# A limit of four filter rows under way in the loads of a convolution that runs beside attention

## The chip, the cores and the metric

The kernel runs on one core of a Trainium2 chip. The core has a matrix engine (TensorE, PE in the profile; its weight loads are PEld), a vector engine (VectorE, DVE), a scalar engine (ScalarE, ACT), a general engine (GpSimd, POOL) and a sequencer that here only issues transfers (SyncE, SP). SBUF is the memory on the core, PSUM the accumulators of TensorE, HBM the main memory. Transfers between HBM and SBUF (DMAs) are issued by SP, ACT or POOL and carried by 16 DMA engines. Each engine takes its own instructions in order; engines wait for one another, and for DMAs, on semaphores.

The metric is the device time of one execution in microseconds. The time before is 860.05 us, the median of three runs (854.38 to 860.23). The profile comes from one more execution, which took 848.04 us.

## The reference

Two independent blocks are computed on inputs of 2048 x 512 in bfloat16 and set side by side in the output. Block A is attention with 32 heads of width 16. Block B is a gated long convolution: a short filter of four taps, a product, then for each of 512 channels a causal convolution over all 2048 positions, done in the reference with an FFT.

```python
def _A_ref(x, wqkv, wo):
    ...
    scores = jnp.einsum("bhqd,bhkd->bhqk", q, k) * (Dh ** -0.5)
    p = _softmax(scores, axis=-1)
    o = jnp.einsum("bhqk,bhkd->bhqd", p, v)
    return (lambda x, *d: x.transpose(*d))(o, 0, 2, 1, 3).reshape(B, S, D) @ wo

def _B_ref(q, k, v, shift_k, ssm_k, ssm_D):
    ...
    kv = k_shift * v
    ...
    y_f = kv_f * kf_f[None, :, :, :]
    y = (lambda x, s, axes=(-2,-1): jnp.fft.irfft2(x, s=s, axes=axes).astype(jnp.bfloat16))(y_f, (1, L), axes=(1, 2))[:, 0, :S, :]
    y = y + kv * ssm_D[None, None, :]
    return q * y

a = _A_ref(A_x, A_wqkv, A_wo)
b = _B_ref(B_q, B_k, B_v, B_shift_k, B_ssm_k, B_ssm_D)
return jnp.concatenate([a, b], axis=-1)
```

## The kernel before

Both blocks run at the same time on the same core, interleaved in one long order of instructions for each engine. A planner in the source, written in Python, makes that order ahead of time: it carries a model of how long everything takes and appends an instruction to an engine's list when the model says that it fits. What the chip then runs is fixed; only the waits on semaphores decide when each instruction starts.

**Attention.** Scores are made in blocks of 128 keys by 512 queries. TensorE multiplies queries and keys (L787, contraction over 32 rows of the array, three blocks at a time), ACT takes the exponential of two or three blocks in one instruction from PSUM to the tile PT (L794), and TensorE multiplies the result with the values (L862). A part of the blocks has its exponential worked out on DVE and POOL by a polynomial instead (L813, L822, L823). Steps are numbered T; each step has one score group, one exponential, and whatever else fits on TensorE before the exponential of that step ends.

**Convolution.** For every channel d the filter, reversed and padded with 128 zeros, is written once at the start to a scratch area in HBM, kz_scratch, as a row of 2176 elements. A *filter row* in SBUF is made from it by one DMA of 128 x 2048 elements: partition p gets the same row shifted by p elements (a Toeplitz matrix). This is `load_wr`, and the tile WR holds a ring of R_W = 14 such rows, slot d % 14. The products k_shift * v lie in the tile KV. TensorE works on four channels at once (a *quad*, qd): for each of 16 lags of 128 positions it makes four matmuls of 128 x 128, one for each channel, in four column groups of the array (`conv_lags`, L988). A quad is therefore 64 matmuls and reads four filter rows; 128 quads make the block. A quad is cut into pieces of up to six lags that the planner puts between the attention's matmuls.

**How the rows are loaded.** The first 14 rows are loaded while the products are made, as WR's memory, which holds other data at first, comes free. After that `conv_lags` issues four loads when it has put the last lag of a quad: the slots of the four rows that this quad has read go to the rows 14 places on. The load is issued from SP and waits until TensorE has finished the quad (`h_wrfree`). Each slot has a semaphore of its own, d_wr[r], and `h_wr[d]` is the handle of row d's landing; the first matmuls of a quad wait for its four rows. From the end of the start phase to the end of the kernel SP has nothing else to issue than these loads, and two stores of the output at the very end. Loads and stores of other tiles (the projection weights WOP, the gate input QN, the outputs) go through POOL. The planner models when a row lands only by numbers of its own (`state["wr"]`), not by the handles of the loads.

Of the kernel before, what the change touches and what calls it, by code (L numbers as in the profile page):

```python
# [28 lines left out]
R_W = 14  # L29
# [5 lines left out]
BGB = 7  # L35
N_EARLY = 70
LAGS = 6

# [131 lines left out]
def bass_concat_heads__mha_block__ssm_conv_h3__prompt_kernel(  # L172
# [163 lines left out]
    def at_job(j):  # L336
        return at_of(j.h) if isinstance(j, Job) and j.h is not None else math.inf if isinstance(j, Job) else at_of(j)
# [23 lines left out]
    def dma(eng, dsem, outp, inp, deps=(), transpose=False):  # L361
        h = dsem.add()

        def fn(e):
            f = e.dma_start_transpose if transpose else e.dma_start
            f(outp, inp).then_inc(dsem.sem, 16)  # L366
        eng.op(fn, deps, inc=False)
        return h
# [221 lines left out]
    def kv_chunk(j):  # L590
        b = kvbuf[kv_buf[j]]
        st = {}

        def tap(m):
            in1 = TB[:, m:m + 1, :].broadcast_to([128, 2, D])
            st[m] = dve_job(lambda e: e.tensor_tensor(b[m], b[m], in1, ALU.mult),
                            [h_kv[(j, 0)], h_kv[(j, 1)], h_tb[m]], 750.0, 3000.0)

        def add(m):
            st["a"] = dve_job(lambda e: e.tensor_tensor(b[3], b[3], b[m], ALU.add), [st[m], st[3], st.get("a")], 750.0, 3500.0)  # L600

        def last():
            def then(h):
                h_kvfree[j] = h
                nxt = {4: 1, 3: None, 2: 0}.get(j, j - 3)
                if nxt is not None and nxt >= 0:
                    load_kv(nxt)
                for d in {6: (0, 1), 5: (2, 3), 4: (4, 11), 3: (8, 9, 12, 13), 1: (5, 6, 7)}.get(j, ()):
                    load_wr(d, [h])
                if j == 5:  # L610
                    load_qn(0, [h_kzt[0]], 4, NB)
                    line[0] += 5000.0
                elif j == 0:
                    start_conv(h)
            for i in range(2):
                dve_job(lambda e, i=i: e.tensor_tensor(KV[:, :, NB - 1 - 2 * j - i, :], quads(b[3][:, i, :]), quads(b[4][:, i, :]), ALU.mult),  # L616
                        [st["a"], h_xt[0]], 700.0, 4000.0 + i, then if i else None)
        return [lambda m=m: tap(m) for m in (3, 2)] + [lambda: add(2), lambda: tap(1), lambda: add(1),
                                                       lambda: tap(0), lambda: add(0), last]

    h_kzw = [None]
# [340 lines left out]
    h_wr, h_wrfree, h_qn = {}, {}, {}  # L962
    h_yb, h_yb_in = {}, {}

    def load_wr(d, deps=()):
        r = d % R_W
        deps = [h_kzw[0], *deps] if d < R_W else [h_wrfree[d - R_W]]
        if d < R_W:
            line[0] += 1350.0
        src = bass.AP(tensor=kz_ap.tensor, offset=kz_ap[d, 0].offset, ap=[[1, 128], [1, S]])  # L970
        h_wr[d] = dma(sp, d_wr[r], WR[:, r, :], src, deps)
# [5 lines left out]
    def conv_lags(qd, n0, n1):  # L977
# [16 lines left out]
        if n1 == NB:  # L994
            for c in range(4):
                h_wrfree[4 * qd + c] = h
                if 4 * qd + c + R_W < C:
                    load_wr(4 * qd + c + R_W)
            if kk % 4 == 3:
                half = kk // 4  # L1000
                src = PS[:, BGB, :]
                src = bass.AP(tensor=src.tensor, offset=PS[:, BGB, 127:128].offset,
                              ap=[src.ap[0], [128, 4], [-1, 128]])
                bank_free[BGB] = dve_job(lambda e: e.tensor_copy(YB[:, half, :].rearrange("p (k i) -> p k i", k=4), src),  # L1004
                                         [h, (lambda: h_yb.get(qd // 8 - 1, WAIT)) if qd >= 8 else None])
                h_yb_in[qd // 4] = bank_free[BGB]
# [41 lines left out]
    def start_conv(h):  # L1048
        h_kvc[0] = h
        state["started"] = True  # L1050
        load_wr(10, [h])
        load_qn(0, [h], 0, 4)
        now = at_of(h)
        state["dma"] = max(line[0], now) + 5000.0
        state["wr"] += [now - 1000.0, max(line[0], now) + 2000.0, state["dma"] - 1400.0]
        state["dma"] -= 1400.0
# [36 lines left out]
    def fill(t, limit):  # L1093
        if t + 450.0 < limit and at_job(bank_free[BGB]) <= t:
            state["fill"] += 2
            bank_free[BGB] = pe_op(keep_busy, [bank_free[BGB]], full(512, 2))
# [27 lines left out]
    def emit_lags(T):  # L1124
# [19 lines left out]
        ahead = [(st["wr"][i] + 1500.0 - now) / (NB * (i - st["qd"]) - st["lag"]) for i in range(st["qd"] + 1, len(st["wr"]))]  # L1144
        st["lags"] = min(st["lags"] + (now - st["now"]) / max([PACE] + ahead), 2.0 * LAGS)
        st["now"] = now
        lags = LAGS
        while st["qd"] < C // 4:
# [3 lines left out]
            if n0 == 0 and (st["wr"][st["qd"]] + 1000.0 > t or st["qd"] % 4 == 0 and at_job(bank_free[BGB]) > t):  # L1152
                if st["qd"] % 4 == 0 and lags == LAGS:
                    fill(t, limit)
# [211 lines left out]
```

## Time and profile before

| What | us |
|---|---|
| Median of three runs | 860.05 |
| Lowest and highest of them | 854.38, 860.23 |
| Profiled execution | 848.04 |
| Its span, first to last instruction | 846.3 |

A page of the profile shows the whole execution: the busy time of each engine, the span in 40 slices with the traffic of the DMA engines in each (21.2 us to a slice), the DMA queues with their bytes, the chain of work that ended last, the costliest groups of instructions (each with what its engine waited for just before), and the DMA issues with the time from issue to landing. Other views ask the same trace more closely: the waits of one engine, the instructions on one tile or one source line, a table of busy time for chosen stretches, and the instructions in order of time.

The queue that carries the filter rows is SP's. What SP itself waited for stands in the view of its waits; the columns are the total in us, how often, and the longest:

```profile
SPq L366 <- PE PS L988: 285.6, 79, 7.0
SPq L366 <- PE PS L1112: 100.2, 26, 6.7
SPq L366 <- PE PS L787: 59.8, 16, 5.9
```

All three are the same wait, for TensorE to be done with a quad (L366 is the line of the helper that issues every DMA). The view names the instruction of PE that came last, whichever line it has. No wait of SP for a filter row is in the program before.

### The profile page before, as it was taken

The numbers are of one execution on the slowest core, as the hardware profiler recorded it, in microseconds if no ns is written. First come the engines' busy times: TensorE is split into PE (matmuls) and PEld (weight loads), VectorE is DVE, ScalarE is ACT, GpSimd is POOL, SyncE is SP. The second block draws the span as 40 slices with busy tenths as digits, with TensorE's granted clock in tenths as the row PEclk, the third lists the DMA queues.
The fourth block names the chain that finished last, engine by engine and source line by source line (L and its number), as shares of the span: only waits on it lengthen the run. The fifth ranks groups of instructions, "written<-read, shape, count | busy, mean of one in ns | idle before, by whom it ended". The sixth has DMA issues, their size and how long they took to land.

```text
span 846.3 us, 30017 instructions
## 1 busy us (share of the span) xinstructions
PE 710.1 (84%) x13188; PEld 308.1 (36%) x13232; DVE 799.7 (94%) x1342; ACT 820.7 (97%) x732; POOL 284.4 (34%) x317
## 2 busy tenths in 40 slices
PE   8988988888888878888788888887888888887887
PEld 3322233433333333333333333333333333343332
DVE  3888999999999999999999999999999999999996
ACT  6999999999999999999999999999999999999997
POOL 3221332333333333233333433334233333323331
PEclk9999999999999999999999999999999999999999
DMA  9868589999999999999999999999999999999942
GB/s 313 301 192 294 174 302 334 367 409 406 391 365 352 399 361 377 387 394 324 409 408 343 350 357 407 406 403 391 354 397 380 378 407 375 372 393 391 388 148 75
DMA packets 88436, 295.69 MB, mean 349 GB/s; under 512 B 11126, under 2 KB 19315, under 8 KB 87923
## 3 DMA queue, kind: packets, MB, share of 16 engines
q1 hardware_dynamic: 82386, 280.00, 88.3%
q0 software_dynamic: 3776, 12.58, 4.4%
q8 instruction: 105, 1.72, 0.8%
q10 hardware_dynamic: 2144, 1.18, 0.5%
q14 instruction: 25, 0.20, 0.1%
HBM read 287.31 MB, written 6.42 MB: 347 GB/s over the span
## 4 chain that ended last, share of the span: by engine, by line
ACT 62%; DVE 23%; PE 11%; issue 2%; DMA 1%; ACTq 0%
ACT PT L794 62%; DVE PTD L823 5%; DVE EI L813 5%; DVE EM L822 5%; PE PS L787 4%; DVE WKV L822 4%; PE PS L862 2%; PE PS L519 1%; DVE QT L540 1%; PE PS L988 1%; DMA WKV<-in_A_wqkv_dram 1%; DVE DT L888 1%; PE PS L505 1%; PE PS L512 1%; PE PS L936 1%
## 5 line engine op out<-in xcount | busy, mean ns | idle before, releaser
L794 ACT ACTIVATE PT<-PS 128x1024 bf16<-128x1024 f32 (+1 forms) x726 | 817.2, 1348 | 13.8 <-PE PS L787 12.8
L787 PE MATMUL PS<-QT,KTo 32*128 32x512 bf16 x2048 | 285.7, 386 | 116.3 <-ACT PT L794 96.9
L988 PE MATMUL PS<-WR,KV 128*8 128x128 bf16 (+15 forms) x8192 | 251.5, 220 | 4.4 <-issue 3.9
L988 PEld LDWEIGHTS PS<-WR,KV 128*1 128x1 bf16 (+15 forms) x8192 | 167.2, 87 | 84.3 <-issue 43.7
L289 POOL TENSOR_SCALAR WKV<-EI 128x512 f32<-128x512 uint16 x128 | 123.6, 965 | 221.1 <-DVE EM L822 85.6
L289 POOL TENSOR_SCALAR EM<-EI 128x512 f32<-128x512 uint16 x128 | 123.1, 962 | 219.4 <-DVE WKV L822 90.1
L862 PE MATMUL PS<-PT,VAF 128*32 128x512 bf16 x1792 | 187.8, 391 | 1.6 <-issue 1.1
L813 DVE TENSOR_SCALAR EI<-PS 128x512 int32<-128x512 f32 x256 | 173.5, 678 | 4.0 <-PE PS L787 3.8
L787 PEld LDWEIGHTS PS<-QT,KTo 32*128 32x128 bf16 x2048 | 71.9, 91 | 276.2 <-ACT PT L794 224.3
L822 DVE SCALAR_TENSOR_TENSOR WKV<-WKV 128x512 f32<-128x512 f32 x256 | 171.0, 680 | 1.1 <-POOL WKV L289 0.7
L822 DVE SCALAR_TENSOR_TENSOR EM<-EM 128x512 f32<-128x512 f32 x256 | 170.9, 686 | 0.2
L823 DVE SCALAR_TENSOR_TENSOR PTD<-EI,WKV 128x512 uint16<-128x512 int32 x128 | 87.2, 682 | 0.6
L823 DVE SCALAR_TENSOR_TENSOR PTD<-EI,EM 128x512 uint16<-128x512 int32 x128 | 86.9, 680 | 0.6
L862 PEld LDWEIGHTS PS<-PT,VAF 128*32 128x32 bf16 x1792 | 47.2, 93 | 105.9 <-issue 98.6
L862 PE MATMUL PS<-PTD,VAF 128*32 128x512 bf16 x256 | 76.4, 387 | 0.6
L1112 PE MATMUL PS<-IDN,ZER 128*32 128x512 bf16 x428 | 48.1, 383 | 0.0
L888 DVE STREAM_TRANSPOSE DT<-PS 128x512 f32<-128x512 f32 x31 | 22.1, 711 | 6.4 <-PE PS L862 5.7
L862 PEld LDWEIGHTS PS<-PTD,VAF 128*32 128x32 bf16 x256 | 19.1, 94 | 18.5 <-DVE PTD L823 8.8
L540 DVE TENSOR_TENSOR QT<-PS,MSK 128x1024 bf16<-128x1024 f32 x15 | 18.4, 1224 | 5.7 <-PE PS L505 5.5
L1004 DVE CAST YB<-PS 128x512 bf16<-128x512 f32 x32 | 21.7, 678 | 0.7 <-PE PS L988 0.5
L366 POOL DMA_DIRECT2D WR<-in_B_k_dram x15 | 11.0, 737 | 27.2 <-DVE KV L616 18.7
L366 POOL DMA_DIRECT2D out_dram<-OUTA x12 | 7.1, 593 | 36.1 <-DVE OUTA L948 36.1
(79 smaller groups left out, 301.2 us busy)
## 6 DMA issues: line engine op xcount, KB each, us to landing
WR<-kz_scratch SPq DMA_DIRECT2D x512, 512.0 KB, 8.1
WR<-in_B_k_dram POOLq DMA_DIRECT2D x15, 256.0 KB, 7.6
kz_scratch<-WR SPq DMA_DIRECT2D x1, 2176.0 KB, 8.6
out_dram<-QN POOLq DMA_DIRECT2D x2, 1024.0 KB, 9.1
QT<-in_B_k_dram POOLq DMA_DIRECT2D x7, 256.0 KB, 7.5
out_dram<-OUTA POOLq DMA_DIRECT2D x12, 128.0 KB, 5.7
WR<-in_B_v_dram SPq DMA_DIRECT2D x5, 256.0 KB, 9.2
WR<-in_B_k_dram SPq DMA_DIRECT2D x5, 256.0 KB, 11.7
```

The costliest lines, as they stand in the source:

```text
L289: q.h = pool.op(lambda e: e.tensor_scalar(UB[m % len(UB)], f, PA, PB, ALU.mult, ALU.add), [h, fx.h, free], cost=Beside((h[0], h[1] + 1)))
L540: hh = dve_job(lambda e: e.tensor_tensor(QT[:, qb % 2, 2 * o:2 * o + 2, :], src, MSK[:, :, 0:1].broadcast_to([128, 2, QB]), ALU.mult), [h, ...
L787: ins = e.matmul(PS[:, bank, :], lhsT=KTo[32 * s:32 * s + 32, g // 2, kt * 128:(kt + 1) * 128], rhs=QT[32 * s:32 * s + 32, qb % 2, g, :], ...
L794: h_exp[T] = act.op(lambda e: e.activation(PT[:, T % R_PT, 0:n * QB], PS[:, banks[0]:banks[0] + n, :].rearrange("p b f -> p (b f)"), ACT.E ...
L813: h_fix[i] = job(lambda e: e.tensor_scalar(ei, PS[:, bank, :], FIX_LO, FIX_ADD, ALU.max, ALU.add), [h, h_pair.get(i - 4)], 692.0, end)
L822: js.append(job(lambda e, c=c: e.scalar_tensor_tensor(u, u, c, u, ALU.add, ALU.mult), [js[-1]], 693.0, due + 700.0 * (len(js) - 3)))
L823: js.append(job(lambda e: e.scalar_tensor_tensor(PTD[:, i % 4, :].bitcast(UINT16), ei, 2.0 ** -9, u, ALU.mult, ALU.add), [js[2], (lambda: ...
L862: ins = e.matmul(PS[32 * s:32 * s + 32, pvb(qb * NG + g), :], lhsT=VAF[:, kt, h * VW:h * VW + 32], rhs=rhs, start=first[b], stop=last[b], ...
L888: h_t = dve_job(lambda e: e.transpose(out=dt, in_=PS[:, pvb(n), :]), [h, h_mult.get(n - 2 if n == 2 else n - 1) if n != 1 else None], 717. ...
L988: ins = e.matmul(PS[32 * c:32 * c + NB - n, BGB, 128 * (kk % 4):128 * (kk % 4) + 128], lhsT=KV[:, qd, n:NB, c], rhs=WR[:, d % R_W, 128 * ( ...
L1004: bank_free[BGB] = dve_job(lambda e: e.tensor_copy(YB[:, half, :].rearrange("p (k i) -> p k i", k=4), src), [h, (lambda: h_yb.get(qd // 8 ...
L1112: ins = e.matmul(PS[32 * s:32 * s + 32, pvb(n), :], lhsT=ZER[:, 0:32], rhs=IDN[:, :].rearrange("p (a f) -> p a f", a=1).broadcast_to([128, ...
```

## The change

A constant is added, and one more condition on the load of a row: row d, from the 15th row on, is issued only when row d - 4 has landed. The first 14 rows are loaded as before.

```diff
 LAGS = 6
+ROWS_OUT = 4
...
     def load_wr(d, deps=()):
         r = d % R_W
-        deps = [h_kzw[0], *deps] if d < R_W else [h_wrfree[d - R_W]]
+        deps = [h_kzw[0], *deps] if d < R_W else [h_wrfree[d - R_W], h_wr[d - ROWS_OUT]]
         if d < R_W:
             line[0] += 1350.0
```

No engine's instructions change their order, since the planner's model doesn't know the landing of the rows. What differs is SP's list of waits. Before the change, this is SP's queue from the last of the first 14 rows on; s_pe is TensorE's semaphore, and the two rows after the first stand for one quad's four loads:

```order
36 L366 DMA WR<-kz_scratch 128x2048 [waits s_dve]
37 L366 DMA WR<-kz_scratch 128x2048 [waits s_pe]
38 L366 DMA WR<-kz_scratch 128x2048 x3
39 L366 DMA WR<-kz_scratch 128x2048 [waits s_pe]
40 L366 DMA WR<-kz_scratch 128x2048 x3
```

After the change, the same place; d_wr10 is the semaphore of slot 10:

```order
36 L367 DMA WR<-kz_scratch 128x2048 [waits s_dve]
37 L367 DMA WR<-kz_scratch 128x2048 [waits d_wr10,s_pe]
38 L367 DMA WR<-kz_scratch 128x2048 [waits d_wr11]
39 L367 DMA WR<-kz_scratch 128x2048 [waits d_wr12]
40 L367 DMA WR<-kz_scratch 128x2048 [waits d_wr13]
41 L367 DMA WR<-kz_scratch 128x2048 [waits d_wr0,s_pe]
42 L367 DMA WR<-kz_scratch 128x2048 [waits d_wr1]
```

The loads stand in the same order as before; each of them has a wait of its own now, on the slot four places back, where before three of four had none. This goes on to the last row: 498 loads, rows 14 to 511.

## The prediction

> **What bounds the kernel now.** I read the page first: engine shares, the chain that ended last, the DMA line and the costliest groups.
>
> ```profile
> span 846.3 us, 30017 instructions
> PE 710.1 (84%) x13188; PEld 308.1 (36%) x13232; DVE 799.7 (94%) x1342; ACT 820.7 (97%) x732; POOL 284.4 (34%) x317
> ...
> GB/s 313 301 192 294 174 302 334 367 409 406 391 365 352 399 361 377 387 394 324 409 408 343 350 357 407 406 403 391 354 397 380 378 407 375 372 393 391 388 148 75
> ...
> q0 software_dynamic: 3776, 12.58, 4.4%
> q8 instruction: 105, 1.72, 0.8%
> ...
> ACT 62%; DVE 23%; PE 11%; issue 2%; DMA 1%; ACTq 0%
> ```
>
> ScalarE (ACT) is busy for 97% of the span and carries 62% of the chain: the softmax exponentials are the bound. DMA has 1% of the chain. Yet the DMA line is close to a ceiling: no slice moves more than 409 GB/s, and most of the slices between 100 and 810 us lie between 350 and 409. So a second limit lies just under the first, and the change acts on that second one. The next views are PE's waits and the instructions on the tile WR, the ring of 14 filter rows.
>
> ```profile
> PE PS L787 <- ACT PT L794: 96.9, 226, 1.0
> PE PS L988 <- issue: 3.9, 4, 1.8
> ...
> L988 PE MATMUL PS<-WR,KV x8192: 216/219/314, 102.5 to 823.2; 128*3 128x128 bf16 x18, 128*14 128x128 bf16 x15, 128*7 128x128 bf16 x14, 128*9 128x128 bf16 x14
> L366 SPq DMA_DIRECT2D WR<-kz_scratch x512: 319/434/1733, 47.8 to 807.0; - x171
> ...
> DMA to landing us min/median/max: 3.9/8.1/13.0
> ```
>
> The first row says that TensorE mostly waits for ACT, not the other way. The second is all that the convolution (L988) waits for, and no DMA is named in it. The third gives the demand: 128 groups of four rows in 823.2 - 102.5 = 720.7 us, 5.63 us for four rows. A row is 128 x 4096 bytes = 524 KB, so four are 2.10 MB, and at the 409 GB/s of the best slice they take 5.13 us. The last line gives the rows under way: 8.1 us of landing at four rows per 5.63 us is 8.1 / 5.63 x 4 = 5.8 rows on average. A limit of four therefore bites nearly always; the change can't be without effect on the queue. The question is whether anybody waits for it.
>
> **The change, part by part.** Nothing is removed, and no instruction changes its place on any engine. Added are 498 waits on SP, one for each row from 14 on. Each is a test on a queue that has only these loads to issue: four issues of 0.434 us (median above) are 1.7 of 5.63 us, so the instructions themselves cost nothing, covered by 3.9 us of idle SP; uncovered they would be less than the 0.05 us of wake-up shown next, for each row. Queued behind a waiting load are only later loads of rows, and at the very end two stores of the output; the last row is issued at 807.0 us, long before those. POOL's DMAs stand in a queue of their own and are not held. Who waits for the row is PE at L988, and since PE runs in order, behind it the score matmuls at L787, and behind those ACT.
>
> The cost is thus one of rate. With four rows out, a row is issued when the row four before has landed; if a row takes L from issue to landing, four rows take at least L plus the time from release to issue. That time is read from the end of a group and the next issue:
>
> ```profile
> 409.94 0.55 PE L988 MATMUL PS<-WR,KV 128*3 128x128 bf16 x12
> ...
> 410.54 13.65 SPq L366 DMA_DIRECT2D WR<-kz_scratch  x11
> ```
>
> 409.94 + 0.55 = 410.49, and the issue starts at 410.54: 0.05 us. What L is with exactly four out, the trace does not show in a steady state, so it is bounded by single loads. I took the loads that open a batch with exactly three earlier rows not yet landed: 17 of them, from 4.2 to 7.2 us, median 5.67. The row at 107.5 met an empty queue; the next three are of the 17 (the one at 801.8 is the median, the one at 161.2 the worst):
>
> ```profile
> L366 SPq DMA_DIRECT2D WR<-kz_scratch x1: 320/320/320, 107.5 to 107.5; - x1
> ...
> DMA to landing us min/median/max: 4.1/4.1/4.1
> ...
> L366 SPq DMA_DIRECT2D WR<-kz_scratch x1: 320/320/320, 801.8 to 801.8; - x1
> ...
> DMA to landing us min/median/max: 5.7/5.7/5.7
> ...
> L366 SPq DMA_DIRECT2D WR<-kz_scratch x1: 319/319/319, 161.2 to 161.2; - x1
> ...
> DMA to landing us min/median/max: 7.2/7.2/7.2
> ```
>
> Low end, L = 4.1: the row's own transfer is 5.13 / 4 = 1.28 us of that, the fixed part 2.8 us. Three rows ahead are 3.85 us of transfer, more than 2.8, so the engines would never run dry, four rows would still take 5.13 us, less than the 5.63 asked for, and the cost is 0. High end, L = 7.2: 7.25 - 5.63 = 1.62 us per four rows, times 498 / 4 = 124.5, is 202 us. A gain isn't in these bounds: rows that land no earlier can't shorten anything. I take the median, 5.67, because those 17 loads are the state that the change makes permanent, while the empty queue of 107.5 is one it never sees, and the load at 161.2 stands behind a 512 KB load of other data (its row comes below). This gives 5.67 + 0.05 - 5.63 = 0.09 us per four rows, 124.5 x 0.09 = **+11.2 us**.
>
> That the rate falls when the queue is shallow, and not only the waiting, is seen by comparing stretches with a deep queue (first two) with stretches just after the queue had run low:
>
> ```profile
> 425.00:435.00 10.00, 3.98 (x4) 1.00 1.03 406
> 436.00:444.00 8.00, 2.01 (x3) 1.00 1.02 408
> 138.50:143.50 5.00, 0.91 (x2) 1.00 0.98 300
> 392.50:400.00 7.50, 2.08 (x2) 1.00 0.86 253
> 654.00:661.00 7.00, 2.62 (x5) 1.00 0.94 277
> 725.50:731.00 5.50, 1.99 (x2) 1.00 0.97 316
> 801.50:807.00 5.50, 1.53 (x2) 1.00 1.01 363
> ```
>
> The last column is GB/s, the one before it the busy share of the DMA engines. In the later rows the engines count as nearly as busy (0.86 to 1.01) while they move 10 to 40% less: single packets take longer there. Each such stretch follows a lull and lasts a few us, so it is not a steady rate; it is the reason why I don't take the low end.
>
> Against this stands a cushion: rows land before they are used.
>
> ```profile
> L366 SPq DMA_DIRECT2D WR<-kz_scratch x1: 443/443/443, 399.9 to 399.9; - x1
> ...
> DMA to landing us min/median/max: 9.8/9.8/9.8
> ...
> 412.19 0.72 PE L988 MATMUL PS<-WR,KV 128*16 128x128 bf16 x24
> ...
> L366 SPq DMA_DIRECT2D WR<-kz_scratch x1: 1467/1467/1467, 491.3 to 491.3; - x1
> ...
> DMA to landing us min/median/max: 12.2/12.2/12.2
> ...
> 503.64 0.51 PE L988 MATMUL PS<-WR,KV 128*16 128x128 bf16 x24
> ```
>
> The first row lands at 409.7 and is used at 412.19, 2.5 us ahead; the second at 503.5 for 503.64, nearly late already. Over the 124 groups after the first four the tightest is 0.2, the median 3.7 us. The cushion is spent once, and the smaller figure counts because the tighter groups come in runs: **-2.5 us**. Last, POOL's transfers share the engines:
>
> ```profile
> WR<-kz_scratch SPq DMA_DIRECT2D x512, 512.0 KB, 8.1
> ...
> out_dram<-QN POOLq DMA_DIRECT2D x2, 1024.0 KB, 9.1
> ...
> out_dram<-OUTA POOLq DMA_DIRECT2D x12, 128.0 KB, 5.7
> ...
> WKV<-in_A_wo_dram POOLq DMA_DIRECT2D x1, 512.0 KB, 7.7
> ```
>
> The last row is the transfer that the load at 161.2 stands behind. The stores of OUTA, 12 of 128 KB at 409 GB/s are 0.32 us each, 3.9 us together. Now they fit into the spare 0.5 us per group (5.63 - 5.13); at 5.72 us there is none: **+3.9 us**, between 0 (the 17 loads hold some of it already) and 9.0 us (with the two stores of QN, 2.1 MB, besides).
>
> Sum: 11.2 - 2.5 + 3.9 = +12.6 us. The profiled execution took 848.04 us (span 846.3 and 1.7 around it), 1.4% under the median of the runs shown, 860.05 (854.38 to 860.23). From 848.04 the sum leads to 860.6; set on the median it is 872.7, and I state that, rounded to 872.5.
>
> A rule of the Trainium skill speaks for the low end: "DMA: Bandwidth & Descriptors", section "Anatomy of one DMA — SWDGE (gpsimd) path", fits a DMA as 2.0 us plus its bytes at 436 GB/s. By it this row would be an estimated 3.2 us, four of them 4.8 us, and the limit free. The trace has 4.1 us for an empty queue and 5.67 with three ahead, and no slice above 409 GB/s, so both terms are too small here; the fit is for the other kind of queue besides. The same page's "Rules for kernel authors" says to issue a DMA early and wait for it late; by that the change goes the wrong way, as in my forecast.
>
> **The rivals.** *The pacing is hidden.* The mechanism is the low end above: three rows ahead (3.85 us) cover the fixed 2.8 us, the engines stay full, and rows wait in SP's queue for as long as they now wait in the DMA queue, landing at the same moment. For it: the 406 and 408 GB/s of the deep stretches show that nothing but the transfer limits there, and PE shows no wait for a row. Against: the five shallow stretches. It decides as long as L + 0.05 stays under 5.63. Change 0, with tight groups such as the one at 503.64 late by some tenths, up to +5: 860 to 865 us. This is the rival on the other side, not slower.
>
> *The shallow rate becomes permanent.* If pacing holds the engines in the state of 725.5 to 731.0, four rows take 2.10 MB / 316 GB/s = 6.64 us, 1.01 us over demand, times 124.5 = +126 us: 986 us. Against: those stretches come after lulls, and with PE waiting there would be no lulls.
>
> *Faster.* Rows issued one at a time in place of bursts of four keep the packets short, and PE loses its waits at L988. Their whole is 3.9 us, so 856 us; a gain over 1% (8.6 us) has no row behind it except what ACT might gain by chance.
>
> **How the numbers follow.** Forecast, +5 to +41 us (the upper bound is the mean of the 17 loads, 5.91: 0.33 x 124.5): 0.50. Hidden: 0.36. Permanent shallow rate: 0.09. Faster: 0.05. About 1%, 8.6 us here, is what a measurement of this kernel can tell from no change. Of the forecast about 0.07 falls under that bound, and of the hidden case 0.03 over it; so faster 0.05, same 0.33 + 0.07 = 0.40, slower 0.43 + 0.03 + 0.09 = 0.55. The range, 856 to 905 us, holds the hidden case, its small losses and the forecast up to a little over its mean-load bound (901), and leaves out the permanent shallow rate and a real gain. The forecast's own range is 865 to 901.
>
> **What would show it.** Right: the median landing of a row falls from 8.1 to about 5.7 us; SP waits for its own rows (the releaser reads DMA WR); PE shows waits of some tenths at L988 on DMA WR, in sum about 10 us; the groups of four come every 5.7 us, and the span grows by what the convolution grows. The hidden case shows a landing near 5.2 us, best slices still at 400 GB/s or more, and no DMA wait at L988. Wrong in size: a landing of 6.5 us or more and slices that never pass 330 GB/s. Wrong altogether: a shorter span with L988 unchanged; then ACT or PE gained from something that this trace doesn't show.

## The result and the profile after

The median is 923.15 us (917.66 to 934.58, 6 runs) against 856.06 us (853.51 to 860.23, 6 runs) before: a ratio of 1.0764 with a 95% interval of 1.0703 to 1.0825. The change makes the kernel 7.6% slower. The profiled execution took 917.66 us.

The first fence has lines of the page: busy time by engine, the traffic in 40 slices (22.9 us each), the queue that fetches TensorE's instructions, the chain that ended last, two groups, and the issues of the rows.

```profile
span 915.9 us, 30142 instructions
...
PE 750.4 (82%) x13188; PEld 314.8 (34%) x13232; DVE 805.3 (88%) x1342; ACT 830.7 (91%) x732; POOL 284.3 (31%) x317
...
GB/s 316 264 249 242 193 340 330 350 337 331 332 350 353 348 349 334 339 346 346 338 351 346 352 351 348 358 334 315 363 352 336 339 329 331 337 333 355 359 264 70
...
q8 instruction: 105, 1.72, 0.7%
...
DMA 84%; ACT 6%; PE 6%; DVE 2%; issue 1%; ACTq 0%; SPq 0%
...
L989 PE MATMUL PS<-WR,KV 128*8 128x128 bf16 (+15 forms) x8192 | 265.2, 227 | 70.1 <-DMA WR<-kz_scratch 68.4
...
L795 ACT ACTIVATE PT<-PS 128x1024 bf16<-128x1024 f32 (+1 forms) x726 | 827.1, 1256 | 73.7 <-PE PS L788 72.2
...
WR<-kz_scratch SPq DMA_DIRECT2D x512, 512.0 KB, 6.2
```

(Every line of the source below the added constant is one further down: L988 is now L989, L787 is L788, L794 is L795.) The chain has turned over: DMA carried 1% of it and ACT 62%, now DMA carries 84%. A row lands sooner, in 6.2 us at the median in place of 8.1, and yet the traffic is lower: in the middle of the span no slice passes 363 GB/s, where the kernel before reached 409. That is what a limit on rows under way does when it binds.

The instructions on the tile WR give the pace of the convolution, and those on kz_scratch the loads and their landing:

```profile
L989 PE MATMUL PS<-WR,KV x8192: 216/219/315, 102.1 to 892.9; 128*3 128x128 bf16 x18, 128*6 128x128 bf16 x15, 128*13 128x128 bf16 x15, 128*7 128x128 bf16 x14
```

```profile
L367 SPq DMA_DIRECT2D WR<-kz_scratch x512: 319/320/1062, 47.4 to 882.3; - x171
...
DMA to landing us min/median/max: 3.8/6.2/13.1
```

892.9 - 102.1 = 790.8 us, 6.18 us for four rows, where it was 720.7 and 5.63. The convolution grew by 70.1 us, and the span by 915.9 - 846.3 = 69.6: all of the loss lies here. Who waits stands in the three views of waits, of PE, of ACT and of SP (total us, times, longest):

```profile
PE PS L989 <- DMA WR<-kz_scratch: 68.4, 65, 3.1
PE PS L788 <- ACT PT L795: 63.9, 156, 1.0
```

```profile
ACT PT L795 <- PE PS L788: 72.2, 106, 3.0
```

```profile
SPq L367 <- DMA WR<-kz_scratch: 452.7, 368, 3.5
SPq L115 <- DMA WR<-kz_scratch: 144.7, 125, 3.5
...
SPq L367 <- PE PS L989: 11.3, 24, 2.3
```

PE waits 68.4 us for rows, a wait that the view of before doesn't have, and its waits for ACT fall from 96.9 to 63.9. ACT waits 72.2 us for scores. SP spends 597.4 us waiting for its own rows (L115 is the helper's line for a wait that stands alone) and hardly any for TensorE. The chain of waits in order of time (start, length, what) shows the loop itself, row d, row d + 4, row d + 8:

```profile
400.68 6.63 DMA WR<-kz_scratch
407.31 0.02 issue
407.33 6.00 DMA WR<-kz_scratch
413.33 0.02 issue
413.35 5.68 DMA WR<-kz_scratch
419.03 0.02 issue
```

From landing to issue go 0.02 us. Over rows 40 to 511 the trace's landings give a mean of 6.23 us from issue to landing and 1.562 us between one landing and the next, four times 6.25 us, 336 GB/s; 494 of the 498 limited rows were issued with exactly three others out. So the pace is the landing time over four, as the prediction had it. What has to be explained is why that time is 6.2 and not 5.7.

### The profile page after: what moved, and what is told of

It reads as the page before. It is cut to its first block, busy times and chain, and to the rows that moved or that the text cites. A ratio compares the mean times of both kernels' runs of the same rounds, so it can differ in the third digit from the quotient of the medians.

```text
span 915.9 us, 30142 instructions
## 1 busy us (share of the span) xinstructions
PE 750.4 (82%) x13188; PEld 314.8 (34%) x13232; DVE 805.3 (88%) x1342; ACT 830.7 (91%) x732; POOL 284.3 (31%) x317
## 3 DMA queue, kind: packets, MB, share of 16 engines
q8 instruction: 105, 1.72, 0.7%
## 4 chain that ended last, share of the span: by engine, by line
DMA 84%; ACT 6%; PE 6%; DVE 2%; issue 1%; ACTq 0%; SPq 0%
DMA WR<-kz_scratch 84%; ACT PT L795 6%; PE PS L788 2%; PE PS L520 1%; PE PS L513 1%; PE PS L863 1%; PE PS L660 0%; DVE EI L814 0%; DVE EM L823 0%; DVE KTo L551 0%; PE PS L989 0%; DVE PTD L824 0%; DVE WKV L823 0%; PE PS L672 0%; DVE QT L601 0%
## 5 line engine op out<-in xcount | busy, mean ns | idle before, releaser
L795 ACT ACTIVATE PT<-PS 128x1024 bf16<-128x1024 f32 (+1 forms) x726 | 827.1, 1256 | 73.7 <-PE PS L788 72.2
L788 PE MATMUL PS<-QT,KTo 32*128 32x512 bf16 x2048 | 297.9, 403 | 79.0 <-ACT PT L795 63.9
L989 PE MATMUL PS<-WR,KV 128*8 128x128 bf16 (+15 forms) x8192 | 265.2, 227 | 70.1 <-DMA WR<-kz_scratch 68.4
L989 PEld LDWEIGHTS PS<-WR,KV 128*1 128x1 bf16 (+15 forms) x8192 | 170.1, 90 | 173.5 <-issue 139.1
L814 DVE TENSOR_SCALAR EI<-PS 128x512 int32<-128x512 f32 x256 | 175.5, 686 | 51.6 <-PE PS L788 51.0
L863 PE MATMUL PS<-PT,VAF 128*32 128x512 bf16 x1792 | 196.3, 409 | 0.9 <-DVE DT L889 0.4
L788 PEld LDWEIGHTS PS<-QT,KTo 32*128 32x128 bf16 x2048 | 72.2, 91 | 237.3 <-ACT PT L795 162.8
L863 PE MATMUL PS<-PTD,VAF 128*32 128x512 bf16 x256 | 79.9, 412 | 1.4 <-DVE PTD L824 0.8
L367 POOL DMA_DIRECT2D WR<-in_B_k_dram x15 | 11.0, 740 | 27.0 <-DVE KV L617 18.7
```

What stands on the lines that cost most here:

```text
L788: ins = e.matmul(PS[:, bank, :], lhsT=KTo[32 * s:32 * s + 32, g // 2, kt * 128:(kt + 1) * 128], rhs=QT[32 * s:32 * s + 32, qb % 2, g, :], ...
L795: h_exp[T] = act.op(lambda e: e.activation(PT[:, T % R_PT, 0:n * QB], PS[:, banks[0]:banks[0] + n, :].rearrange("p b f -> p (b f)"), ACT.E ...
L814: h_fix[i] = job(lambda e: e.tensor_scalar(ei, PS[:, bank, :], FIX_LO, FIX_ADD, ALU.max, ALU.add), [h, h_pair.get(i - 4)], 692.0, end)
L863: ins = e.matmul(PS[32 * s:32 * s + 32, pvb(qb * NG + g), :], lhsT=VAF[:, kt, h * VW:h * VW + 32], rhs=rhs, start=first[b], stop=last[b], ...
L989: ins = e.matmul(PS[32 * c:32 * c + NB - n, BGB, 128 * (kk % 4):128 * (kk % 4) + 128], lhsT=KV[:, qd, n:NB, c], rhs=WR[:, d % R_W, 128 * ( ...
```

## The experiments

Two explanations were set against each other first. One: four rows of 512 KB are too few to keep 16 DMA engines busy, whatever else runs. The other: four would do, but other traffic on the same engines makes some rows land late, and with only four out nothing covers it.

**Rows alone.** Everything but the loads is left out, attention and convolution too; rows are loaded in stretches of 56 with n out at most (the second number 1 means that each partition reads a row of its own in HBM in place of one row shifted by an element from partition to partition).

```diff
+PHASES = [(1, 0), (2, 0), (3, 0), (4, 0), (5, 0), (6, 0), (8, 0), (12, 0), (4, 1), (12, 1)]
...
+    for n, spread in PHASES:
...
+            if i >= n:
+                deps.append(h_wr[d - n])
...
+            h_wr[d] = dma(sp, d_wr[d % R_W], WR[:, d % R_W, :], src, deps)
```

> Only the filter-row loads, nothing else: ten stretches of 56 rows each with at most 1, 2, 3, 4, 5, 6, 8, 12 rows under way, then 4 and 12 again with every partition reading a row of its own in HBM (the whole of attention and convolution is left out). Theory 1 (a row is landed when the slowest of the 16 DMA engines is done; the others run dry meanwhile, so four rows cannot cover the fixed part plus the spread): the single row takes 4.0 us; with 4 under way the four take clearly more than 5.1 us, up to 6.2, also in this empty machine. Theory 2 (the other traffic of the kernel, POOL's transfers and the fetches of instructions, makes the delay): here four rows take 5.1 to 5.3 us with 4 under way, 408 GB/s, and only 1 to 3 rows under way are slower. Theory 3 (all engines read the same 4 KB of HBM at once): Theory 1's 6 us for the Toeplitz rows, but 5.1 to 5.3 us where each partition reads its own row.

The windows lie inside the stretches with 1, 2, 3, 4 and 5 out; the columns are the window, its length, POOL's busy time, PE's clock, the busy share of the DMA engines, and GB/s:

```profile
60.00:221.00 161.00, 0.00 (x0) 1.00 0.44 150
250.00:340.00 90.00, 0.00 (x0) 1.00 0.74 249
360.00:445.00 85.00, 0.00 (x0) 1.00 0.89 286
460.00:520.00 60.00, 0.00 (x0) 1.00 1.03 410
535.00:595.00 60.00, 0.00 (x0) 1.00 1.03 410
```

Four rows reach 410 GB/s, and no deeper queue does better. By the landings four rows take 5.14 us there with a landing of 5.10 us; a row alone lands in 3.47 us. Own rows in HBM change nothing with four out (5.14). So the first explanation falls for four rows (it holds for three, 286 GB/s): what stretches the landing to 6.2 us is something that the whole kernel has and this one has not.

**Five rows.** `ROWS_OUT` is the only thing that differs.

```diff
-ROWS_OUT = 4
+ROWS_OUT = 5
```

> A limit of five rows. If the landing time of a row stays what it is with four (6.2 us), five rows give 6.25 / 5 x 4 = 5.0 us per quad, under the demand of 5.63: no wait at L989 to speak of, 856 to 862 us. If a shallow queue itself slows the packets, the rate rises only from 336 to some 350 GB/s, 6.0 us per quad, +0.4 x 124.5 = +46 us: about 900 us.

851.97 us against 855.08, ratio 0.9957 (0.9925 to 0.9989). The loss is gone. The views of PE's waits and of kz_scratch:

```profile
PE PS L788 <- ACT PT L795: 95.9, 224, 1.0
PE PS L989 <- issue: 3.8, 3, 2.0
```

```profile
DMA to landing us min/median/max: 3.9/6.6/12.9
```

No wait for a row is left, and PE's wait for ACT is back (96.9 before). In the chain of its profile ACT carries 72% and DMA 1%: a single row more turns the DMA-bound kernel back into the ACT-bound one.

**Three rows.** The same constant, 3, to see whether the pace follows the depth.

> A limit of three rows. With a landing time that hardly depends on the depth (between 5.5 and 6.2 us), a quad takes 7.3 to 8.3 us: +210 to +335 us over the 848 of the profiled run, 1060 to 1185 us. If the rate is what counts and the landing time scales with the depth (6.2 x 3 / 4 = 4.7 us), the quad stays at 6.25 us and the time at about 920 us.

1079.74 us, in a single run, as the first of the two expectations had it: the landing hardly gets shorter, and the pace follows the depth. Four rows take 7.565 us (277 GB/s) with a landing of 5.6 us, and PE's wait is:

```profile
PE PS L989 <- DMA WR<-kz_scratch: 176.8, 90, 5.6
```

**Rows of their own.** The limit stays at four; each partition of a load reads another row of HBM, so that the convolution gets other filter values. In the kernel the 128 partitions read nearly the same 4 KB.

```diff
-        src = bass.AP(tensor=kz_ap.tensor, offset=kz_ap[d, 0].offset, ap=[[1, 128], [1, S]])
+        src = bass.AP(tensor=kz_ap.tensor, offset=kz_ap[d % 384, 0].offset, ap=[[LKZ, 128], [1, S]])
```

> The limit of four with one thing else: partition p reads its own row of the scratch area, 128 rows of HBM in place of one row shifted (the convolution's filter values are thereby other ones). If the engines hinder each other on the same 4 KB, the landing falls to 5.2 us and the time to about 856 us. If not, it stays at 6.2 us and about 920 us.

882.39 us (877.08 to 887.7, two runs), ratio to before 1.0342 (1.0253 to 1.0431): between what the two sides expected. Four rows take 5.97 us, the landing 5.8.

```profile
PE PS L788 <- ACT PT L795: 74.4, 174, 1.0
PE PS L989 <- DMA WR<-kz_scratch: 36.7, 37, 2.4
```

About half of the loss goes when no address is shared, although sharing costs nothing when four rows run alone. Both fit if something disturbs the engines and the shared address makes the disturbance worse. The edit changes two things at once, though: the addresses are no longer shared, and each partition's read starts 4352 bytes behind the last one's (a row of 2176 elements) in place of 2. No run parts the two; "shared address" stands for both below.

**What the disturbance is, from the trace.** I sorted the intervals between two landings of rows by the time since the last fetch of instructions began on a DMA queue (rows near a transfer of POOL's left out). The figures are computed from the packets and landings in the traces of before and after:

```
us since a fetch    before: mean interval (rows)   after: mean interval (rows)
0-2                 1.300 (124)                    1.436 (112)
2-4                 1.427 (127)                    1.888 (103)
4-8                 1.365 (161)                    1.420 (178)
over 8              1.507 (12)                     1.560 (30)
```

Over 1.28 us, the time of a row at full rate (5.13 / 4), the intervals 2 to 4 us behind a fetch add up to 62.6 us after and 18.7 before, all others to 50.8 and 18.9. Of the increase of 76 us, 44 stand right behind a fetch. The line q8 of the page gives the size: 105 packets of 16 KB hold 0.7% of 16 engines' span, 0.007 x 16 x 915.9 / 105 = 0.98 us each, on one engine, some 7 us apart. The section "Instruction fetch mechanics" of the Trainium skill's page "Runtime: NRT & Kernel Launch" says that an engine's instructions come in blocks of 16 KiB, 256 instructions, on a DMA queue of its own, and that this is mostly hidden. For TensorE the trace agrees with the first: 13188 + 13232 instructions over 256 are 103. (The packets of the other fetch queue, q14, hold 8 KB.) As for hidden, no line of PE's waits after has more than 2.0 us on `issue`; what the table shows delayed is the transfers beside the fetch.

**One engine held, on purpose.** Rows alone again, and with every fifth row POOL moves 16 KB on one DMA engine.

```diff
+PHASES = [(1, 1, 0), (2, 1, 0), (3, 1, 0), (3, 0, 0), (4, 0, 0), (4, 0, 1), (5, 0, 1), (8, 0, 1), (4, 1, 1)]
...
+                    h_hit = dma(pool, d_hit, HIT[0:1, 0:8191], x1[0:1, 0:8191], [h_wr[d - 8], h_hit])
```

> The bare loads without a stream of instructions (attention and convolution are left out). First 1, 2, 3 rows under way with every partition reading its own row, then 3 and 4 as in the kernel; then 4, 5 and 8 as in the kernel and 4 with own rows, each with an added transfer of 16 KB by one DMA engine for every fifth row, issued by POOL. If engines that run dry are slow because all read the same 4 KB: the first three stretches are faster than the 13.96, 8.47 and 7.33 us for four rows measured with shared rows (3 under way: near 5.2). If they are slow for want of work alone: the same figures again. The added transfers, about 1 us of one engine each: with 4 under way four rows go from 5.14 to 5.5 or more, with 8 they stay under 5.4, if a single late engine is what holds the row.

The windows are three rows with own addresses, three shared, four undisturbed, then disturbed four, five, eight and four with own rows (columns as above):

```profile
382.00:466.00 84.00, 0.00 (x0) 1.00 0.91 315
485.00:578.00 93.00, 0.00 (x0) 1.00 0.88 283
593.00:658.00 65.00, 0.00 (x0) 1.00 1.03 409
674.00:748.00 74.00, 4.42 (x9) 1.00 0.99 359
762.00:833.00 71.00, 4.69 (x9) 1.00 1.02 387
844.00:918.00 74.00, 4.69 (x9) 1.00 0.99 393
934.00:1004.00 70.00, 4.69 (x9) 1.00 1.01 387
```

By the landings four rows take 5.12 us undisturbed; disturbed they take 5.89 with four out, 5.50 with five, 5.53 with eight, 5.44 with four of their own. The fifth row and the separate addresses each take away a part, as in the kernel. But with eight out the expectation was under 5.4, and it failed. The landings tell why: each load raises its semaphore 16 times, once for each engine, and has landed with the last. That last report comes 0.37 us behind the one before it with four out, 1.19 with five and 2.88 with eight, in the mean (0.16 undisturbed). A lag that grows with the queue means that one engine gets all the added transfers and sets the pace, whatever the depth: if each engine carries 32 KB of a row, 16 KB more on one engine for five rows is a tenth, an estimate of 5.12 x 1.1 = 5.6 us. So this run shows that 16 KB on one engine delays rows that are four deep; it is no copy of the kernel, where a fifth row covers everything. One and two rows with own addresses were no faster than in the first experiment (14.00 and 8.83 us against 13.96 and 8.47): those two depths are slow for want of work, three rows in part for the shared address (6.64 against 7.32).

**Real fetches, of two engines.** Rows alone beside streams of small instructions that do nothing for the rows: 11,000 on VectorE and 8,000 on TensorE.

```diff
+PHASES = [(4, 0), (5, 0), (6, 0), (12, 0), (4, 1), (5, 1), (3, 1)]
...
+    for i in range(N_DVE):
+        dve.op(lambda e, i=i: e.memset(TINY[:, 2 * i:2 * i + 2], 0.0), inc=False)
+    for i in range(N_PE):
+        pe.op(lambda e: e.matmul(PSB[:, 0:128], lhsT=MMW[:, :], rhs=MMW[:, :], start=True, stop=True), [hm], inc=False)
```

> The bare loads again, while VectorE and TensorE run through some 19,000 tiny instructions of no use, so that the instruction queue fetches its 16 KB packets as it does in the whole kernel (attention and convolution are left out). Stretches of 72 rows with 4, 5, 6, 12 rows under way, then 4, 5 and 3 with every partition reading its own row. Theory 2a (each fetch holds one DMA engine for 1.0 us; with four rows under way the others run dry behind it): with 4 under way the four rows rise from 5.14 us to 5.6 or more, and the delay comes in the landings 2 to 4 us after a fetch; with 6 and 12 they stay under 5.35. Rival (POOL's transfers, or the compute engines' own traffic on the memory on the core, do it): with fetches alone it stays at 5.14 to 5.25 us in all of them.

The page has the two fetch queues, and the windows (PE's busy time in the middle) are four, five and six rows out:

```profile
q8 instruction: 62, 1.02, 0.5%
q14 instruction: 90, 0.74, 0.2%
```

```profile
45.00:142.00 97.00, 97.00 (x1741) 1.00 0.97 336
155.00:256.00 101.00, 101.00 (x1813) 1.00 0.97 341
270.00:372.00 102.00, 102.00 (x1830) 1.00 0.95 337
```

Four out gave the kernel's rate at once: 6.23 us for four rows. But five and six gave 6.20 and 6.25, where the kernel with five has no loss, and the expectation failed there. In those two stretches the last of the sixteen engines comes in 1.64 and 2.97 us after the last but one, in the mean over their rows (0.34 with four out): as with the added transfers, one engine has more to do than the others and sets the pace; why it has so much more is open. This run has 90 fetches on q14, VectorE's here; the kernel's q14 has 26. By itself the run decides nothing, so the two streams were parted.

**Real fetches, TensorE's alone.**

```diff
-N_DVE, N_PE = 11000, 8000
+N_DVE, N_PE = 1, 14000
...
-PHASES = [(4, 0), (5, 0), (6, 0), (12, 0), (4, 1), (5, 1), (3, 1)]
+PHASES = [(4, 0), (5, 0), (6, 0), (12, 0), (4, 1), (3, 0)]
```

> The bare loads beside a stream on TensorE alone, 14,000 small matmuls of no use, whose instructions are fetched in packets of 16 KB some 7 us apart, as in the whole kernel (attention and convolution are left out). In the run with two streams a limit of four gave 6.23 us per four rows, but five and six gave 6.20 and 6.25 with a single DMA engine 3 to 4 us behind the rest, so a second thing was in play there, presumably the added 8 KB fetches of VectorE. Stretches of 72 rows: 4, 5, 6, 12, then 4 with own rows, then 3. If fetches and too shallow a queue together make the delay: 4 gives 5.7 to 6.3 us, 5 at most 5.5, 6 and 12 at most 5.4. If one engine bears all the fetches and sets the rate: about the same figure, near 6.0, at 4, 5, 6 and 12. If the fetches of TensorE do nothing: 5.14 everywhere.

The queue of TensorE's fetches, and the windows in the order of the stretches, 4, 5, 6, 12 out, 4 with own rows, 3:

```profile
q8 instruction: 109, 1.79, 0.9%
```

```profile
45.00:142.00 97.00, 97.00 (x1741) 1.00 0.97 335
155.00:240.00 85.00, 85.00 (x1526) 1.00 1.01 398
255.00:338.00 83.00, 83.00 (x1490) 1.00 1.01 399
350.00:436.00 86.00, 86.00 (x1545) 1.00 1.01 400
450.00:542.00 92.00, 92.00 (x1652) 1.00 0.98 367
560.00:680.00 120.00, 120.00 (x2153) 1.00 0.87 277
```

Set beside the whole kernels, four rows taking so many us:

```
                          rows alone   with TensorE's fetches   whole kernel
4 out                     5.14         6.19                     6.25
4 out, own rows           5.14         5.73                     5.97
3 out                     7.33         7.56                     7.565
5 out                     5.12         5.22                     no wait for rows (demand 5.63)
```

With nothing added but TensorE's small matmuls and the fetches that they need, the rows go within 0.1 us of the kernel's pace with four and with three out. With own rows 0.24 us of the kernel's pace is missing; what adds it there wasn't tried. No engine lags for good (the last comes 0.53 us behind the last but one with four out, 0.25 with five), but the engines fall out of step: from the first to the last of the sixteen reports of a row it is 0.67 us with four rows alone and 2.27 beside the fetches. TensorE is busy through every window, also where the rows run at 398 to 400 GB/s, so its work alone is not what slows them. And the same sorting of intervals in this run, which has hardly any other traffic:

```
us since a fetch    4 out         5 out         4 out, own rows
0-2                 1.450 (13)    1.268 (16)    1.261 (14)
2-4                 1.727 (21)    1.370 (20)    1.823 (17)
4-6                 1.451 (19)    1.277 (17)    1.322 (20)
over 6              1.478 (10)    1.277 (10)    1.261 (12)
```

With five out, the rows behind a fetch lose 0.1 us and the rest run at full rate. With four out and own addresses, the rows behind a fetch lose about 0.5, and the next ones are back at full rate. With four out and the shared address, the mean doesn't come back to full rate before the next fetch. So the loss has two parts: the engine that a fetch holds, and a slow return to full rate that only the shared address shows.

**Six rows, and five once more.** The constant again, 6 and 5, the latter with more rounds, since five had come out below the kernel before.

> A limit of six rows. With five the time was 0.4% under the kernel before. If that gain is from a limit as such (fewer rows queued), six gives part of it, 0.996 to 1.000; if five still costs something at the fetches and gains elsewhere, six is a little better than five, 0.993 to 0.997. Either way no wait at L989 on a row.

> The limit of five again, in more rounds, since its ratio of 0.9957 (0.9925 to 0.9989) lay just under one and six gave 1.0023. If the gain is real: 0.993 to 0.998. If it was the chip of that run: an interval that holds 1.

Six: 856.88 us, ratio 1.0023 (0.9986 to 1.006), landing 7.6 us and no wait for a row; the time is in neither of the two ranges expected. Five: 850.43 us against 853.87, ratio 0.9954 (0.9915 to 0.9993), with one wait of 1.5 us for a row in the profile. Twice the interval of five lies just under 1, by some 0.45%; that is too small to call the kernel faster, and where it comes from is open. The granted clock of TensorE was higher with five, 0.986 and 0.987 in the means of the two runs against 0.982 before, and the executions of one kernel differ by about 6 us for 0.01 of clock, so most of the gain goes with the clock. But with six the clock was 0.986 against 0.982, and there was no gain.

## Why the prediction was wrong, step by step

**Right: where the bound lies and who waits.** The limit binds on nearly every row, the landing time over four sets the pace, PE waits at L989 with the releaser DMA WR, ACT behind it, and SP waits for its own rows. The bound of 1.7 us for SP's own work stood: the step from landing to issue takes 0.02 us (0.05 was taken).

**The step that failed: "I take the median, 5.67, because those 17 loads are the state that the change makes permanent".** The permanent landing is 6.23 us. The same formula with it gives 6.23 + 0.02 - 5.63 = 0.62 us, times 124.5 = 77 us, and 70 were seen. The term of 11.2 us was too small by 66; the demand of 5.63 stands so close under the landing that half a microsecond of error in it is nearly all of the result. The mean of the 17 (5.91, +41 us as the upper bound) was short as well. The sample was chosen too narrowly, and the trace of before shows it. In it 25 loads were issued with exactly three rows out; the 17 are those that open a batch. The other 8 were issued within 0.5 us of the load before them and took 7.25 us in the mean. All 25 have a median of 6.19 and a mean of 6.34 us, close to the steady state. Where a batch opens, the three rows ahead are further along: the last of them landed 3.99 us after the issue, in the mean of the 17, and in the steady state it lands after 4.66. That the 25 come so close is partly luck, since they mix two cases and neither is paced. (The prediction announces three of the 17 in its fence; two stand there.)

The steady state itself is made of something for which the prediction has no term. Four rows alone land in 5.10 us; beside the fetches of instructions, each holding one engine for 0.98 us every 7 us or so, they land in 6.1 (medians). A row has landed when its slowest engine has. That the other engines run out of work behind the late one when only four rows are out is my reading, since no view shows the queue of a single engine; what the runs show is that a fifth row covers it (5.22 us for four rows). The shared address is part of it: without it the whole kernel was some 40 us faster (923.15 against 882.39, two runs).

**The low end was right, for an empty machine.** It said that three rows ahead keep the engines full and that four take 5.13 us; the rows alone took 5.14. Its error was to know only one thing that has to be covered, the fixed 2.8 us of a load. By the fit of the Trainium skill's page "DMA: Bandwidth & Descriptors", section "Anatomy of one DMA — SWDGE (gpsimd) path", a row is an estimated 3.2 us; alone it took 3.47, so the fit is near the measurement for one load, and says nothing of an engine that something else holds.

**Cushion, -2.5.** Between the 77 us that the landing gives and the 70.1 measured lie 7 us. In the trace after, the groups of rows 12 to 43 are used 5.0 us after their last row has landed, in the mean, and from row 48 on 0.6 (0.13 at the median). So the cushion spent is some 4.4 us in place of 2.5; the rest was not taken apart.

**POOL's stores, +3.9.** Rows that land within 2 us after a packet of POOL's was started came at 1.717 us after (43 of them), all others at 1.549: 43 x 0.17 = 7 us, an estimate that lies between the bounds of 0 and 9.0. The landing of 6.23 us holds it already. What traffic the engines carry besides was the right question, but it was asked of one queue only: q8 stood in the prediction's first fence, with 1.72 MB, and got no term. Its bytes are few; what it does is hold one engine.

**The rivals.** The pacing was not hidden. The permanent shallow rate, 316 GB/s and 986 us, was put aside because with PE waiting there would be no lulls; measured are 336 GB/s and 923. The objection was wrong: the rows slow down behind each fetch, and that needs no lull in the loads. The result lies between forecast and this rival, and the range ended before it.

**The signs.** The groups come every 6.18 us rather than 5.7, and PE's wait is 68.4 rather than about 10. The test for "wrong in size" asked for a landing of 6.5 and no slice over 330 GB/s; 6.2 and 363 already mean 70 us, since what counts is the 0.5 us between 5.67 and 6.2.

**Not tried.** Issuing the next row when only some of the 16 engines have landed the earlier one, which would say how much of the loss is waiting for the slowest of them, was not run.

## What to carry to other kernels

A limit on transfers under way has to cover more than the time that one transfer takes in an empty machine: it has to cover the time for which something else holds a single DMA engine as well, because a transfer spread over 16 engines lands with the slowest. In this kernel that took one row more. (Where one engine has more to carry all along, as in the run with POOL's transfers, depth beyond five didn't help: 5.50 and 5.53 us with five and eight out.) When a change makes a pace out of a landing time, work out how much the result moves for each 0.1 us of it (here 12 us), take every case that meets the condition into the sample, and if the spread of the sample is larger than the margin, put the range where the spread ends. Before setting such a limit, load the same rows alone and beside a long stream of instructions; one step deeper can be the whole difference.

## What the runs showed of the hardware that was not expected

- Alone, one, two, three and four loads of 512 KB under way move 150, 249, 286 and 410 GB/s; the step from three to four is the largest, and a fifth adds nothing.
- The busy share of the DMA engines hardly falls with the traffic: beside TensorE's fetches it is 0.97 at 335 GB/s and 1.01 at 398. So the packets take longer for the same bytes, and a share near 1 doesn't say how much could still be moved.
- 128 partitions that read nearly the same 4 KB cost nothing while four rows run alone (5.14 us shared and own), but 0.68 us for four rows with three out (7.32 against 6.64), and 0.46 with four out beside fetches (6.19 against 5.73). That it is the sharing, and not where the reads start, isn't shown.
- TensorE's granted clock was lower in the kernels in which it waited more for rows: 0.992 before, 0.961 with own rows, 0.945 after, 0.852 with three rows. In the order of time (start, length, engine, line, what, and in brackets the idle time before) the same three score matmuls take 0.39 us and, after two waits, 0.61:

```profile
407.45 0.29 PE L989 MATMUL PS<-WR,KV 128*16 128x128 bf16 x8 [1.87 <-DMA WR<-kz_scratch]
407.68 0.39 PE L788 MATMUL PS<-QT,KTo 32*128 32x512 bf16 x3
...
409.62 0.61 PE L788 MATMUL PS<-QT,KTo 32*128 32x512 bf16 x3 [0.40 <-ACT PT L795]
```

With DMA at 84% of the chain I don't take it for a part of the loss, but no run held the clock fixed to show that.
